# A first transfer of 512 bytes a partition for w_in, and one transfer instead of two for half of wq

## The chip, the cores and the metric

The kernel runs on one core of one Trainium2 chip. The metric is the device time of one execution in microseconds (us); several runs are made, and their median counts.

## What is computed

One decode step of a block that joins sliding-window attention with a gated MLP. Two batch rows of one token, model width 512, 32 query heads over 8 key/value heads of width 128, and a window of the last W = 4096 positions of a cache of 32768. All data are float32.

```python
def reference(A_x, A_k_cache, A_v_cache, A_wq, A_wo, B_x, B_w_in, B_w_sp, B_b_sp, B_w_out):
    x = A_x                                   # 2 x 1 x 512
    xn = _layernorm(x)
    s = _A_ref(xn, A_k_cache, A_v_cache, A_wq, A_wo)
    g = _silu(_B_ref(xn, B_w_in, B_w_sp, B_b_sp, B_w_out))
    return x + s * g

# _A_ref: q = x @ wq (512 x 4096); softmax(q k^T * Dh**-0.5) v over the last W = 4096
#         positions of k_cache, v_cache; then @ wo (4096 x 512)
# _B_ref: z = gelu(x @ w_in) (512 x 1792); z1, z2 = halves; z2 = layernorm(z2);
#         (z1 * (w_sp * z2 + b_sp)) @ w_out (896 x 512)
```

Nearly all of the data are the window of K and V: 2 x 8 x 4096 x 128 values each, 67 MB together. The weights wq and wo have 8.4 MB each, w_in 3.7 MB and w_out 1.8 MB.

## The kernel before

**Loads.** All large loads are issued from SP's queue, in program order. They go through a ring of four tiles of 32 KB a partition (`slot`, line 111) that w_in, the two halves of wq, the K and V units and wo take in turn; a load into a slot waits until the slot's former contents have been used. First come w_in (line 122, 28,672 bytes a partition), w_out (line 124, into a pool of its own, `kts`, which has two buffers), and wq (lines 127 to 131) as two tiles of two rows of wq a partition: the first tile in one transfer of 32 KB a partition, the second in two transfers of 16 KB. Then K and V follow (`load`, line 146) as 8 units of 4 MB each, and six pieces of wo at the end. ScalarE's queue issues the four tiny loads (x twice, w_sp, b_sp).

**The head of the work.** x is normalised and transposed (xn, xnT). PE multiplies it with w_in as soon as that has landed (z, lines 236 to 248), then transposes z back (zT). `queries(k)` (line 263) multiplies xnT with one row tile of wq, 16 matmul instructions each: queries(0) and queries(1) use the first wq tile, queries(2) and queries(3) the second, and k is the accumulation over PSUM, so that the queries are complete after queries(3). Between them stand the small matmuls of the gating branch (mean, variance). After queries(3) PE multiplies with w_out (y), ScalarE copies the queries out (qs), VectorE transposes them (qx) and masks them (xm), PE spreads them (qa), and `place_queries` (the step `q`) lays them out in qb, which every score needs. The buffers of qs and qx are those of `kts`, which afterwards hold the transposed K.

**The units.** The order of everything afterwards is written out by hand in `ORDER` (lines 27 to 52); each word is a step, and each engine runs its steps in that order. For unit u: `K:u` and `V:u` issue the loads; `T:u.0` to `T:u.7` are the 8 transposes of K on VectorE (STREAM_TRANSPOSE, 128x1024); `shares`, `keep` and `scores` are the score matmuls with a copy on ScalarE between them; `rowmax`, `mg`, `shmax` and `bias` give the softmax's maximum; `exp` and `probs_t` the probabilities and their transpose; `pv` multiplies with V (acc); `evac` and `col` gather the heads. Units overlap: while unit u+1 is transposed, unit u's probabilities and `pv` run. `K:0 K:1 V:0` stand first, then `K:2 V:1` with unit 1, and so on; the last loads are those of `wo:0` and `wo:1`.

**The end.** X, Y and U multiply with wo into `part`, Z adds the last rows of wo into `so`, and two VectorE operations multiply with the gate and add x (`res`).

The helper class `InOrder` records every instruction of PE, DVE, ACT and SP, and so nearly all of them show its line (L65) in the profile; they are told apart by their tiles.

Of the kernel before, what the change touches and what calls it, by code (L numbers as in the profile page):

```python
# [70 lines left out]
def kernel(  # L71
# [14 lines left out]
    pe, dve, act, sp = (InOrder(tc, e) for e in (nc.tensor, nc.vector, nc.scalar, nc.sync))  # L86
# [24 lines left out]
    def slot(name, *shape):  # L111
        return ring.tile([P, *shape], F32, tag="slot", name=name)
# [6 lines left out]
    act.dma_start(xs, x[:, 0, :])  # L119
    win_v = w_in.rearrange("(p k) f -> p k f", p=P)  # L120
    win = slot("win", KT, F)
    sp.dma_start(win, win_v)
    wout = kts.tile([P, FT, D], F32, tag="kts", name="wout")
    sp.dma_start(wout, w_out.rearrange("(p j) d -> p j d", p=P))
    wq_v = wq.rearrange("(p k) f -> p k f", p=P)
    wqt = []
    for a in range(0, KT, 2):
        t = slot(f"wq{a}", 2, HQ * DH)
        for k, n in ((0, 2),) if a == 0 else ((0, 1), (1, 1)):
            sp.dma_start(t[:, k : k + n], wq_v[:, a + k : a + k + n, :])  # L130
        wqt += [t[:, 0], t[:, 1]]

    wb1 = cst.tile([1, 2], F32, tag="wb1", name="wb1")
# [92 lines left out]
    for nj in (8, 16):  # L226
        nx = 32 // nj
        to = cst.tile([P, nj * P // 32 // 4, 4, nx], F32, tag=f"perm{nj}", name=f"perm{nj}")
# [374 lines left out]
    for u in range(NU):  # L603
        p = Unit()
        p.u, p.m, p.kt, p.sh, p.ss, p.s, p.p, p.pT = u, None, {}, {}, {}, {}, {}, {}
        units.append(p)
    for line in ORDER.strip().split("\n"):
        for name in line.split():
            name, at = name.split(":")
            u, _, a = at.partition(".")  # L610
# [34 lines left out]
```

## Time and profile before

| | |
|---|---|
| Median of 3 runs | 216.89 us (216.76 to 216.92) |
| Profiled execution: its own time | 217.29 us |
| Profiled execution: span from the first to the last instruction | 215.5 us |
| Mean granted TensorE clock | 0.825 |
| HBM read | 89.40 MB, 415 GB/s over the span |
| Busy: PE, DVE, ACT | 66%, 59%, 24% of the span |

How it is read: all times inside the profile are in us from the start of the span of that one execution, which took 0.4 us longer than the median run. The 16 DMA engines each work through their own share of every load in the order in which SP issued them, 8 of the 128 partitions' rows each; a load is landed when all 16 are done.

### The profile page before, as it was taken

The page shows a single profiled execution, that of the slowest core. Times are in us where ns is not written, and L with a number is a line of the kernel's source. Part 1 is how long each engine was busy: PE and PEld are TensorE (multiplying, and loading weights), DVE is VectorE, ACT ScalarE, POOL GpSimd, SP SyncE. Part 2 cuts the span into 40 slices and gives each one's busy share as a digit, 9 for nine tenths or more (in the row PEclk, how much of TensorE's full clock was granted, in tenths as well). Part 3 has the DMA queues.
Part 4 walks back from the last instruction along what each step waited for, and adds up shares of the span by engine and source line. Part 5 has one row for each costly group of instructions (what it writes and reads, how often), then busy time and mean ns, then how long its engine had stood idle before and what let it go on. Part 6 is the DMA issues. An engine that isn't in the chain of part 4 may idle for free.

```text
span 215.5 us, 2332 instructions
## 1 busy us (share of the span) xinstructions
PE 143.2 (66%) x900; PEld 48.1 (22%) x900; DVE 126.7 (59%) x218; ACT 51.6 (24%) x129; POOL 4.5 (2%) x17
## 2 busy tenths in 40 slices
PE   0179796833854966964991795389259917987793
PEld 0117622111120221222220231123112201232231
DVE  2611213169899799649928972993698099636011
ACT  5011103300116036033330602142051206142201
POOL 8000000000000000000000000000000000000000
PEclk9999569665998896796697599669755997996999
DMA  7999999999999999999999999999999999999990
GB/s 246 432 443 444 398 429 465 414 458 414 456 408 447 420 426 444 426 443 426 450 420 450 408 441 420 426 450 426 447 415 456 401 456 414 447 426 417 420 374 22
DMA packets 3930, 89.54 MB, mean 416 GB/s; under 512 B 446, under 2 KB 462, under 8 KB 848
## 3 DMA queue, kind: packets, MB, share of 16 engines
q1 hardware_dynamic: 3900, 89.40, 96.8%
q8 instruction: 7, 0.11, 0.2%
q14 instruction: 3, 0.02, 0.0%
q10 hardware_dynamic: 20, 0.01, 0.0%
HBM read 89.40 MB, written 0.00 MB: 415 GB/s over the span
## 4 chain that ended last, share of the span: by engine, by line
DMA 63%; PE 23%; DVE 8%; ACT 3%; issue 1%; ACTq 0%
DMA v<-in_A_v_cache_dram 42%; DMA k<-in_A_k_cache_dram 16%; PE acc L65 10%; DMA win<-in_B_w_in_dram 5%; PE sh L65 5%; DVE kts L65 4%; PE part L65 4%; PE s L65 3%; DVE pT L65 1%; ACT p L65 1%; ACT o L65 1%; DVE gate L65 1%; PE mo L65 1%; ACT ss L65 1%; DVE qb L65 1%
## 5 line engine op out<-in xcount | busy, mean ns | idle before, releaser
L65 DVE STREAM_TRANSPOSE kts<-k 128x1024 f32<-128x1024 f32 x64 | 75.6, 1218 | 29.5 <-DMA k<-in_A_k_cache_dram 29.5
L65 PE MATMUL sh<-kts,qb 128*32 128x512 f32 x256 | 41.6, 775 | 13.2 <-DVE kts L65 9.3
L65 PE MATMUL acc<-v,pT 128*32 128x512 f32 x256 | 37.4, 707 | 8.8 <-DVE pT L65 4.4
L65 ACT ACTIVATE p<-s,nb 128x512 f32<-128x512 f32 x32 | 22.5, 733 | 36.2 <-DVE nb L65 36.2
L65 ACT ACTIVATE ss<-sh 128x512 f32<-128x512 f32 x16 | 9.6, 599 | 59.1 <-PE sh L65 59.1
L65 DVE STREAM_TRANSPOSE pT<-p 128x1024 f32<-128x1024 f32 x16 | 19.6, 1225 | 2.3 <-ACT p L65 2.1
L65 PE MATMUL s<-ss,sums 128*128 128x512 f32 x32 | 18.8, 671 | 2.3 <-ACT ss L65 2.3
L65 PE MATMUL mo<-mg,joint 128*128 128x16 f32 x16 | 4.0, 327 | 23.4 <-DVE mg L65 23.4
L65 PEld LDWEIGHTS acc<-v,pT 128*32 128x32 f32 x256 | 10.5, 145 | 35.1 <-issue 27.0
L65 PEld LDWEIGHTS sh<-kts,qb 128*32 128x32 f32 x256 | 8.8, 126 | 34.2 <-issue 28.8
L65 DVE TENSOR_REDUCE m<-s 128x1 f32<-128x512 f32 x16 | 10.7, 671 | 4.2 <-PE s L65 4.2
L65 PE MATMUL q_ps<-wq,xnT 128*32 128x512 f32 x64 | 10.5, 784 | 3.5 <-DMA wq<-in_A_wq_dram 3.5
L65 ACT ACTIVATE o<-acc,wd 128x128 f32<-128x128 f32 x32 | 9.1, 368 | 15.0 <-PE acc L65 15.0
L65 PEld LDWEIGHTS mo<-mg,joint 128*128 128x128 f32 x16 | 3.2, 250 | 27.2 <-DVE mg L65 24.4
L65 PE MATMUL z<-win,xnT 128*32 128x448 f32 x32 | 5.6, 869 | 4.7 <-DMA win<-in_B_w_in_dram 4.7
L65 PE MATMUL part<-wo,oT 128*32 128x512 f32 x56 | 7.7, 596 | 1.4 <-ACT o L65 1.4
L65 PEld LDWEIGHTS s<-ss,sums 128*128 128x128 f32 x32 | 5.0, 197 | 10.3 <-issue 7.7
L65 PE MATMUL zT_ps<-rowm,z 128*128 128x2 f32 x28 | 6.6, 370 | 0.0
L65 PEld LDWEIGHTS zT_ps<-rowm,z 128*128 128x128 f32 x28 | 6.5, 325 | 0.0
L65 ACT ACTIVATION_READ_ACCUMULATOR p<-s,nb 128x1 f32 x32 | 6.5, 203 | 0.0
L65 ACT ACT_TABLE_LOAD x4 | 5.1, 1283 | 2.6 <-POOL hT L164 2.6
L65 DVE COPY z<-z 128x448 f32<-128x448 f32 x2 | 1.3, 626 | 7.5 <-PE z L65 7.5
(111 smaller groups left out, 68.4 us busy)
## 6 DMA issues: line engine op xcount, KB each, us to landing
k<-in_A_k_cache_dram SPq DMA_DIRECT2D x8, 4096.0 KB, 27.4
v<-in_A_v_cache_dram SPq DMA_DIRECT2D x8, 4096.0 KB, 29.8
wq<-in_A_wq_dram SPq DMA_DIRECT2D x1, 4096.0 KB, 24.5
wq<-in_A_wq_dram SPq DMA_DIRECT2D x2, 2048.0 KB
wo<-in_A_wo_dram SPq DMA_DIRECT2D x1, 4096.0 KB, 30.4
win<-in_B_w_in_dram SPq DMA_DIRECT2D x1, 3584.0 KB, 11.5
wo<-in_A_wo_dram SPq DMA_DIRECT2D x1, 2048.0 KB
wout<-in_B_w_out_dram SPq DMA_DIRECT2D x1, 1792.0 KB, 15.3
```

Source lines behind the costliest of these rows:

```text
L65: return self.tc.keep_in_program_order(call(*args, **kwargs))
```

## The change

w_in's load becomes two transfers from the same queue: the first moves the first 128 floats (512 bytes) of every partition's row, the second the other 28,160 bytes. The second tile of wq, which was loaded in two transfers of 16 KB a partition, is loaded in one of 32 KB. The number of transfers stays the same, and so do all other instructions and their order.

```diff
     win_v = w_in.rearrange("(p k) f -> p k f", p=P)
     win = slot("win", KT, F)
-    sp.dma_start(win, win_v)
+    FIRST = 128
+    of, to = win_v.rearrange("p k f -> p (k f)"), win.rearrange("p k f -> p (k f)")
+    sp.dma_start(to[:, :FIRST], of[:, :FIRST])
+    sp.dma_start(to[:, FIRST:], of[:, FIRST:])
     wout = kts.tile([P, FT, D], F32, tag="kts", name="wout")
     sp.dma_start(wout, w_out.rearrange("(p j) d -> p j d", p=P))
     wq_v = wq.rearrange("(p k) f -> p k f", p=P)
     wqt = []
     for a in range(0, KT, 2):
         t = slot(f"wq{a}", 2, HQ * DH)
-        for k, n in ((0, 2),) if a == 0 else ((0, 1), (1, 1)):
-            sp.dma_start(t[:, k : k + n], wq_v[:, a + k : a + k + n, :])
+        sp.dma_start(t, wq_v[:, a : a + 2, :])
         wqt += [t[:, 0], t[:, 1]]
```

## The prediction

> **What bounds the kernel now.** I read the page first, then the chain that ended last, then the DMA's share in short windows at both ends of the span, then the timelines of SP's queue, PE and DVE. The page's slices and its queue list say that this is a kernel of loads.
>
> ```profile
> span 215.5 us, 2332 instructions
> ...
> DMA  7999999999999999999999999999999999999990
> GB/s 246 432 443 444 398 429 465 414 458 414 456 408 447 420 426 444 426 443 426 450 420 450 408 441 420 426 450 426 447 415 456 401 456 414 447 426 417 420 374 22
> ...
> q1 hardware_dynamic: 3900, 89.40, 96.8%
> ```
>
> The 16 DMA engines are busy in every slice but the first and the last, and one queue (SP's) fills 96.8% of them. 89.40 MB at the usual 425 GB/s or so is 210 us of the 215.5. Only the ends are left: slice 0 moved 246 GB/s.
>
> The chain that ended last (start, length, what) shows how the rest hangs on this stream:
>
> ```profile
> 0.73 11.48 DMA win<-in_B_w_in_dram
> ...
> 12.23 33.92 DMA k<-in_A_k_cache_dram
> ...
> 150.21 32.33 DMA v<-in_A_v_cache_dram
> 182.54 0.14 issue
> 182.68 1.95 PE acc L65 x16
> ...
> 206.95 3.64 PE part L65 x28
> ...
> 212.61 0.29 DVE res L65
> ```
>
> A V load that was issued at 150.21 lands at 182.54, although 4 MB need only about 10 us of the stream: it stood 22 us behind other loads. From that landing to 212.9 the chain is compute alone. So the end is the place of that load in the stream plus some 30 us, and a stream that runs d us earlier from its start ends the kernel d earlier. The other end of the stream agrees. In windows (columns: stretch, length, busy time with count of PE, PEld, DVE, ACT, POOL, then clock, DMA share, GB/s):
>
> ```profile
> 0.00:1.60 1.60, 0.00 (x0) 0.00 (x0) 0.00 (x0) 0.00 (x0) 1.05 (x10) 1.00 0.00 0
> 1.60:2.60 1.00, 0.00 (x0) 0.00 (x0) 0.95 (x3) 0.04 (x1) 1.00 (x4) 1.00 1.86 463
> 2.60:3.20 0.60, 0.00 (x0) 0.00 (x0) 0.53 (x3) 0.60 (x1) 0.60 (x1) 1.00 0.00 0
> 3.20:4.20 1.00, 0.00 (x0) 0.00 (x0) 0.01 (x1) 0.97 (x3) 1.00 (x4) 1.00 0.94 401
> 4.20:5.20 1.00, 0.00 (x0) 0.00 (x0) 0.00 (x0) 1.00 (x1) 0.81 (x3) 1.00 1.07 459
> ...
> 207.00:209.00 2.00, 2.00 (x18) 0.71 (x20) 0.00 (x0) 0.00 (x0) 0.00 (x0) 1.00 1.00 407
> ...
> 211.00:211.50 0.50, 0.43 (x19) 0.17 (x12) 0.00 (x0) 0.27 (x1) 0.00 (x0) 1.00 0.09 33
> ...
> 211.57 0.65 PE L65 MATMUL so<-wo,oT 128*32 128x128 f32 x16
> ```
>
> The last pieces of wo are still moving after 211, and the matmuls that need them (the last row, from PE's timeline) are PE's last. Both ends of the work are therefore tied to the stream, not to a free engine.
>
> The same rows hold the term on which this prediction turns. A packet is counted in the window in which it starts. In 1.60:2.60 the rate 463 GB/s over 1 us is 463 KB: 16 rows of w_in of 28,672 bytes, one for each DMA engine, and 4 KB of x. They occupy 1.86 x 16 = 29.8 engine-us, so 1.86 us a row. In 4.20:5.20 again 16 rows start (459 KB) and occupy 1.07 x 16 = 17.1, so 1.07 us a row. Between them, from 2.60 to 3.20, no row starts at all. So **each engine's first row costs 0.79 us more than a later one**, a toll that is paid once, at the head of the stream on which all hangs.
>
> **The change part by part.** The SP queue's timeline, and two of the waits on it:
>
> ```profile
> 0.73 0.39 SPq L65 DMA_DIRECT2D win<-in_B_w_in_dram  x1
> 1.18 0.41 SPq L65 DMA_DIRECT2D wout<-in_B_w_out_dram  x1
> 1.63 1.76 SPq L65 DMA_DIRECT2D wq<-in_A_wq_dram  x3
> 12.23 6.27 SPq L65 DMA_DIRECT2D k<-in_A_k_cache_dram  x2
> ...
> 39.53 0.54 SPq L65 DMA_DIRECT2D k<-in_A_k_cache_dram  x1
> 56.46 0.54 SPq L65 DMA_DIRECT2D v<-in_A_v_cache_dram  x1
> ...
> SPq L65 <- DMA win<-in_B_w_in_dram: 8.8, 1, 8.8
> ```
>
> *The head.* A transfer of 128 rows of 512 bytes (64 KB) goes first, and the remaining 28,160 bytes a row follow one issue later: 1.18 - 0.73 = 0.45 us. Before, the bulk's first rows start at about 1.85 (middle of the starts in 1.60:2.60) and lose 0.79, as if the stream had begun at full speed at 2.64. After, the bulk starts at about 1.85 + 0.45 = 2.30 and has 64 KB less to move, 0.15 us at 425 GB/s. If the small rows take the toll during that issue, the stream stands as if begun at 2.30 - 0.15 = 2.15: **0.49 us gained**. If the toll returns on the bulk, it stands at 2.94: 0.30 lost. No row shows a transfer of small rows on all engines ahead of a large one in an empty queue, so these are the two sides; the worst is that each pays the toll in turn (small rows done at 1.85 + 0.79 + 0.15, then 0.79 again, less the 0.15): 3.43, 0.79 lost. A landing needs all 16 engines, and the second rows start over more than 1 us (14 of the 16, 401 KB, in 3.20:4.20, the others later), so the slowest engine pays about 0.5 more than the mean; if that goes as well, the gain is 1.0. I take -0.6: the mean toll with a little of the spread, since the toll looks tied to the first data, not to the row's length: from the second row on the rate is full at once.
>
> By the Trainium skill, "DMA: Bandwidth & Descriptors", section "Rules for kernel authors", small transfers are to be coalesced, and under 64 KB one pays mostly overhead; its table of measured bandwidth (another issuing path) gives 0.95 us for 64 KB. By that, as an estimate, the 64 KB would cost 0.80 over their 0.15, and the sum would be 217.7 rather than 216.3. No run here shows such a transfer yet.
>
> *The number of rows.* w_in adds 128 rows, the merged wq takes 128 away; five transfers stand ahead of the first K before and after. What a row or a completion costs beside its bytes cancels.
>
> *K:0's issue.* SP waits 8.8 us for w_in's landing before it issues K:0, into a slot that nobody held: of the DMAs in program order (x, w_in, w_out, three of wq, two scalars, x4, K:0) the tenth seems to wait for the second. The count is the same after, so K:0 would wait for the small piece and go out at about 3.5 instead of 12.23. Worth nothing: K:0 lands at 46.15, so its 10 us of data begin near 36. K:1 behind it takes w_in's slot and waits for z's matmuls, as before.
>
> *The queries.* PE and DVE around them, with the total of DVE's waits for K (us, times, longest) as the last row:
>
> ```profile
> 12.35 5.56 PE L65 MATMUL z<-win,xnT 128*32 128x448 f32 x32 [4.73 <-DMA win<-in_B_w_in_dram]
> ...
> 26.18 3.64 PE L65 MATMUL q_ps<-wq,xnT 128*32 128x512 f32 x16 [1.43 <-DMA wq<-in_A_wq_dram]
> ...
> 32.68 1.92 PE L65 MATMUL q_ps<-wq,xnT 128*32 128x512 f32 x16
> ...
> 36.69 2.79 PE L65 MATMUL q_ps<-wq,xnT 128*32 128x512 f32 x16 [2.09 <-DMA wq<-in_A_wq_dram]
> 39.24 2.79 PE L65 MATMUL y<-wout,hT 128*32 128x512 f32 x14
> 44.27 1.12 PE L65 MATMUL qa<-xm,same 128*128 128x256 f32 x2 [2.25 <-DVE xm L65]
> ...
> 46.17 1.25 DVE L65 STREAM_TRANSPOSE kts<-k 128x1024 f32<-128x1024 f32 x1 [2.05 <-DMA k<-in_A_k_cache_dram]
> 47.34 1.19 DVE L65 TENSOR_TENSOR qb<-qa,grpm 128x1024 f32<-128x1024 f32 x1
> ...
> 75.42 3.50 DVE L65 STREAM_TRANSPOSE kts<-k 128x1024 f32<-128x1024 f32 x3 [1.41 <-DMA k<-in_A_k_cache_dram]
> ...
> 94.75 3.50 DVE L65 STREAM_TRANSPOSE kts<-k 128x1024 f32<-128x1024 f32 x3 [3.89 <-DMA k<-in_A_k_cache_dram]
> ...
> DVE kts L65 <- DMA k<-in_A_k_cache_dram: 29.5, 7, 6.7
> ```
>
> queries(2) runs at 32.68 on the first half of the second wq tile; queries(3) waits for the other half until 36.69. Merged, both wait until about 36.7. PE then has 16 matmuls more to do behind the landing: 1.92 us at the pace of 32.68, 3.64 at that of 26.18. Queued behind them on PE are y and qa; SP's K:2 at 39.53 waits for the last one too. qa ends at 45.39, and would end at 47.3 to 49.0; qb starts at 47.34 because DVE is busy with the first transpose of K:0. So qb slips by 0 to 1.7 us and the transposes behind it with it. That slip dies at DVE's next waits for K: 1.41 us at 75.42, 3.89 at 94.75. The loads issued late are covered as well: K:2 (39.53 plus up to 3.6) lands at 75.4 and its data start 10 us before; V:1 (56.46 plus up to 1.7) comes behind K:2 in the stream. Price nil. Without that cover the whole 1.7 would reach the end.
>
> *Sum.* The profiled execution took 217.29 us, its span 215.5 and 1.8 around it; the median of the runs is 216.89, 0.4 lower. 217.29 - 0.6 = 216.7 for a profiled execution, **216.3 for the median**.
>
> **The rivals.** *The toll returns (slower).* The small transfer is through before the bulk's rows are there, the engines start from an empty queue a second time, and the bulk is one issue late: +0.30 to +0.79, 217.2 to 217.7, middle 217.4. For it: in an empty queue every engine paid, all 16 alike, and 64 KB are 0.15 us of work against an issue slot of 0.45, so the queue does run dry if the small rows go at full speed. Against it: then the small rows paid nothing, and a queue that was in use 0.2 us before isn't a cold one. It decides from the point where the bulk loses over 0.49 us on its first rows. The rule named above speaks for this side.
>
> *Nothing moves.* The slow stretch up to about 3 us is fixed in time, whatever is in the queue (no row starts from 2.60 to 3.20); the small piece and the later issue both lie inside it: 216.9, 0.15 either way. The landings then keep their places.
>
> *The queries' slip isn't absorbed.* If PE runs both queries and y at its slow pace and DVE's waits for K vanish, up to 1.7 us reach the end: 218.6. Against it stand DVE's seven waits for K, 29.5 us in all, the longest 6.7: the slip would have to outlast each of them.
>
> **How the numbers follow.** The three runs before lie within 0.07%; 0.2%, 0.43 us, is about what a measurement can tell. Toll absorbed 0.44 (all of it faster by over 0.2%). Toll returns 0.38: about a third of it, 0.12, below +0.43, so 0.26 slower. Nothing moves 0.14. Slip not absorbed 0.04. Hence faster 0.44, same 0.26, slower 0.30. The forecast's own range is 215.8 to 216.45 (-1.1 to -0.43); with the other cases on both sides holding over half the chance, the range goes to 217.6, which leaves out the dearest end of the returning toll and the slip.
>
> **What would show it.** Right: in windows at the head, 64 KB of small rows near 1.6 to 1.9, then rows of 28,160 bytes at 1.05 us each from about 2.3, and no empty stretch like 2.60:3.20; z's matmuls start some 0.5 us before 12.35; the DVE waits for K at 75.42 and 94.75 end 0.5 earlier, and the V landing that was at 182.54 also. K:0's issue stands near 3.5, queries(2) and (3) run back to back from about 36, and that leaves no mark after 95. Wrong: the bulk's first rows again at 1.8 us (the toll returned), z later than 12.35; or landings that moved while the end did not, which would mean that the last 30 us aren't tied to the stream.

## The result, and the profile after

| | Median | Range | Runs |
|---|---|---|---|
| Before | 216.85 us | 216.60 to 216.98 | 13 |
| After | 217.21 us | 216.97 to 217.84 | 13 |

The changed kernel is slower by 0.36 us, by the medians; the ratio of the runs is 1.0021 (+0.46 us) with a 95% interval of 1.0012 to 1.0029, which is +0.26 to +0.63 us. That is inside the stated range and on the other side of the forecast of -0.6: the rival "the toll returns" is what happened, at the low end of its price.

The profiled execution of the changed kernel took 217.06 us with a span of 215.3; that of before took 217.29 with 215.5. Taken alone, these two would say "faster". But before's profiled execution was slower than the slowest of its 13 runs, and one profiled execution against another can't show 0.2%. The sign comes from the medians, and the profiles serve for the places.

SP's queue and PE after the change:

```profile
0.73 0.86 SPq L65 DMA_DIRECT2D win<-in_B_w_in_dram  x2
1.63 0.50 SPq L65 DMA_DIRECT2D wout<-in_B_w_out_dram  x1
2.18 1.28 SPq L65 DMA_DIRECT2D wq<-in_A_wq_dram  x2
3.51 14.39 SPq L65 DMA_DIRECT2D k<-in_A_k_cache_dram  x2
...
12.51 4.78 PE L65 MATMUL z<-win,xnT 128*32 128x448 f32 x32 [4.88 <-DMA win<-in_B_w_in_dram]
```

w_out is issued at 1.63 instead of 1.18, one slot of 0.45 us later, so w_in's bulk went out near 1.18. K:0 is out at 3.51 instead of 12.23. z starts at 12.51 instead of 12.35. The head in windows (stretch, length, PE, PEld, DVE, ACT, POOL, clock, DMA share, GB/s):

```profile
1.60:2.20 0.60, 0.00 (x0) 0.00 (x0) 0.55 (x3) 0.00 (x0) 0.60 (x4) 1.00 0.40 116
2.20:3.20 1.00, 0.00 (x0) 0.00 (x0) 0.93 (x4) 0.61 (x1) 1.00 (x1) 1.00 1.70 451
3.20:4.40 1.20, 0.00 (x0) 0.00 (x0) 0.03 (x1) 1.17 (x3) 1.20 (x4) 1.00 0.61 258
```

The first row holds the small piece: 116 GB/s over 0.6 us is 70 KB (64 KB of w_in and x), in 0.40 x 0.6 x 16 = 3.8 engine-us (us summed over the 16 engines), about 30 ns for each of the 130 rows. At the full rate worked out below they would take 2.6, so they paid 0.08 us an engine: hardly any toll. In the second row the 16 first rows of the bulk start (451 KB), and they occupy 1.70 x 16 engine-us, 1.70 us each, where at full rate (459 KB in 17.1 engine-us before, 26.8 KB per us and engine) they would take 1.05. The toll is back on them, 0.65 us, and they start some 0.5 us later than before: none starts before 2.20, where 14 of the 16 had started by then (676 GB/s in the same 0.6 us from 1.60, 406 KB). Two signs that the prediction had named for being wrong are there: the bulk's first rows again near 1.8 us (1.70), and z later than 12.35 (12.51; by itself this proves little, since with the merge of wq alone, below, z starts at 12.01). The small piece bought next to nothing.

VectorE's waits for K after the change, against 75.42, 94.75, 114.06 and 133.43 of before where such a wait is shown:

```profile
75.83 3.50 DVE L65 STREAM_TRANSPOSE kts<-k 128x1024 f32<-128x1024 f32 x3 [0.29 <-DMA k<-in_A_k_cache_dram]
95.19 3.50 DVE L65 STREAM_TRANSPOSE kts<-k 128x1024 f32<-128x1024 f32 x3 [4.91 <-DMA k<-in_A_k_cache_dram]
...
172.76 1.25 DVE L65 STREAM_TRANSPOSE kts<-k 128x1024 f32<-128x1024 f32 x1 [6.09 <-DMA k<-in_A_k_cache_dram]
```

K lands 0.41 and 0.44 later. In this pair of executions the last one, at 172.76, is earlier than before's:

```profile
152.73 1.25 DVE L65 STREAM_TRANSPOSE kts<-k 128x1024 f32<-128x1024 f32 x1 [5.24 <-DMA k<-in_A_k_cache_dram]
172.91 1.25 DVE L65 STREAM_TRANSPOSE kts<-k 128x1024 f32<-128x1024 f32 x1 [6.66 <-DMA k<-in_A_k_cache_dram]
```

Between these two waits of before lie 20.2 us, where the other steps from K to K are 19.3 to 19.4 (75.42, 94.75). Before's profiled execution lost some 0.8 us there. What did it isn't shown; it would account for the two spans standing the wrong way round.

The queries after the change, and qb behind them:

```profile
37.10 6.37 PE L65 MATMUL q_ps<-wq,xnT 128*32 128x512 f32 x32 [3.43 <-DMA wq<-in_A_wq_dram]
43.29 1.89 PE L65 MATMUL y<-wout,hT 128*32 128x512 f32 x14
...
48.59 1.23 DVE L65 TENSOR_TENSOR qb<-qa,grpm 128x1024 f32<-128x1024 f32 x1 [0.15 <-PE qa L65]
```

queries(2) and (3) run back to back from 37.10, qb is 1.25 us late (48.59 against 47.34), and 0.29 of VectorE's 1.41 us wait at the third K is left; at the next K it waits 4.91 us.

### The profile page after: what moved, and what is told of

It reads as the page before. It is cut to its first block, busy times and chain, and to the rows that moved or that the text cites. A ratio compares the mean times of both kernels' runs of the same rounds, so it can differ in the third digit from the quotient of the medians.

```text
span 215.3 us, 2332 instructions
## 1 busy us (share of the span) xinstructions
PE 140.4 (65%) x900; PEld 48.0 (22%) x900; DVE 126.7 (59%) x218; ACT 51.6 (24%) x129; POOL 4.5 (2%) x17
## 4 chain that ended last, share of the span: by engine, by line
DMA 55%; PE 20%; DVE 18%; ACT 3%; issue 2%; SPq 1%; DVEq 0%; ACTq 0%
DMA k<-in_A_k_cache_dram 25%; DMA wq<-in_A_wq_dram 16%; DMA wo<-in_A_wo_dram 15%; DVE kts L65 12%; PE sh L65 5%; PE acc L65 4%; PE part L65 4%; PE q_ps L65 3%; PE s L65 2%; ACT p L65 2%; DVE pT L65 2%; DVE m L65 1%; PE y L65 1%; SPq L65 1%; DVE gate L65 1%
## 5 line engine op out<-in xcount | busy, mean ns | idle before, releaser
L65 PE MATMUL acc<-v,pT 128*32 128x512 f32 x256 | 34.9, 663 | 8.6 <-DVE pT L65 4.4
L65 PE MATMUL s<-ss,sums 128*128 128x512 f32 x32 | 17.9, 640 | 2.5 <-ACT ss L65 2.5
L65 PE MATMUL q_ps<-wq,xnT 128*32 128x512 f32 x64 | 12.8, 963 | 5.7 <-DMA wq<-in_A_wq_dram 5.7
L65 PEld LDWEIGHTS mo<-mg,joint 128*128 128x128 f32 x16 | 3.4, 263 | 29.6 <-DVE mg L65 26.8
L65 PE MATMUL z<-win,xnT 128*32 128x448 f32 x32 | 4.8, 733 | 4.9 <-DMA win<-in_B_w_in_dram 4.9
L65 DVE STREAM_TRANSPOSE qx<-qs 128x512 f32<-128x512 f32 x2 | 1.3, 690 | 7.9 <-PE y L65 7.9
```

Source lines behind the costliest of these rows:

```text
L65: return self.tc.keep_in_program_order(call(*args, **kwargs))
```

## The experiments

The differences in us are of the medians, against the runs of the kernel before on the same chip; the interval is that of the ratio, times 216.9. Each version has 5 to 12 runs, the kernel before 15 to 29 beside them. Theory A is the returning toll with the later issue, theory B the merged wq, theory C both in part.

**w_in split, wq as before.** One transfer more than before.

```diff
-        sp.dma_start(t, wq_v[:, a : a + 2, :])
+        for k, n in ((0, 2),) if a == 0 else ((0, 1), (1, 1)):
+            sp.dma_start(t[:, k : k + n], wq_v[:, a + k : a + k + n, :])
```

(against the changed kernel)

> w_in begins with the 512-byte transfer, wq stays in its two 16 KB pieces (one transfer more than before). Theory A (the bulk of w_in is issued one slot of 0.45 us late, 0.15 us of it is used, its first rows pay the toll again): the whole loss is here, +0.3 to +0.4 us against the kernel before, the waits for K end 0.4 later, queries(2) runs at about 33 as before. Theory B (the merged wq is the cause, through queries and qb 1.2 us late): within 0.1 us of the kernel before. Theory C (both in part): about +0.2.

Measured 217.40 against 216.87: +0.53, interval +0.43 to +0.91. The whole loss is in the split of w_in; it is somewhat larger than the 0.3 to 0.4 that theory A gave.

**wq merged, w_in as before.**

```diff
-        for k, n in ((0, 2),) if a == 0 else ((0, 1), (1, 1)):
-            sp.dma_start(t[:, k : k + n], wq_v[:, a + k : a + k + n, :])
+        sp.dma_start(t, wq_v[:, a : a + 2, :])
```

(against the kernel before)

> w_in in one transfer as before, the second wq tile in one transfer. Theory A: 0 against the kernel before (within 0.1 us): qb is late by 1 to 2 us, and the waits for K stand at 75.4 and 94.8 as before. Theory B: +0.3 to +0.4 us. Theory C: about +0.2.

Measured 216.94 against 216.87: +0.07, interval -0.13 to +0.26. Theory B falls. Its profile shows the slip and where it ends: qb starts at 47.91, and VectorE waits for K again at 95.05.

```profile
47.91 1.19 DVE L65 TENSOR_TENSOR qb<-qa,grpm 128x1024 f32<-128x1024 f32 x1
...
95.05 3.50 DVE L65 STREAM_TRANSPOSE kts<-k 128x1024 f32<-128x1024 f32 x3 [3.35 <-DMA k<-in_A_k_cache_dram]
```

That wait ends 0.30 later than before's 94.75 although the kernel is no slower, so a single landing of K carries 0.3 us of scatter from one execution to another. The landings above support the medians; alone they would prove little.

**A first piece of 4096 bytes a partition.** `FIRST = 1024` instead of 128 in the changed kernel.

> As the change, with a first piece of 4096 bytes a partition instead of 512 (512 KB, 1.2 us of the stream, more than the issue slot of 0.45 us). Theory A: the bulk's rows are queued before the engines run out of the first piece, so the later issue costs nothing and the toll is paid once: 0 against the kernel before (within 0.1 us), first K wait back at about 75.4. Theory B: +0.3 to +0.4 as the change. If every separate first transfer costs a fixed sum, whatever its size: +0.3 to +0.4 too, but with the waits for K late.

Measured 216.65 against 216.87: -0.22, interval -0.39 to 0.00. The loss is gone, though the bulk is issued as late as in the change. Whether 0.2 us were gained beyond that is the question of the last experiment. The head in windows:

```profile
1.60:3.35 1.75, 0.00 (x0) 0.00 (x0) 1.40 (x4) 0.78 (x1) 1.75 (x4) 1.00 0.86 241
3.35:4.40 1.05, 0.00 (x0) 0.00 (x0) 0.17 (x2) 1.02 (x3) 1.05 (x4) 1.00 1.16 476
```

The first stretch moves 422 KB (the first piece, mostly) in 24.1 engine-us, 15.7 of which are the bytes at full rate: 8.4, or 0.52 us an engine, is the toll. In the second stretch, where the bulk's first rows start, 500 KB take 19.5 engine-us, 25.6 KB per us and engine: within 5% of full rate. With 4 KB rows the first piece pays the toll, and the bulk doesn't pay again.

**Two pieces of 512 bytes ahead of the bulk.**

```diff
     sp.dma_start(to[:, :FIRST], of[:, :FIRST])
-    sp.dma_start(to[:, FIRST:], of[:, FIRST:])
+    sp.dma_start(to[:, FIRST : 2 * FIRST], of[:, FIRST : 2 * FIRST])
+    sp.dma_start(to[:, 2 * FIRST :], of[:, 2 * FIRST :])
```

(against the changed kernel)

> As the change, with two transfers of 512 bytes a partition one after the other ahead of the bulk. Theory A: the bulk is issued one slot later again, 0.4 to 0.45 us less 0.15 us of bytes: +0.6 to +0.8 us against the kernel before, waits for K at 76.1 or so. Theory B: +0.3 to +0.4 as the change.

Measured 217.78 against 216.87: +0.91, interval +0.59 to +1.13. Each short transfer ahead of the bulk costs about one issue slot of 0.45 (w_out, behind the bulk, is issued at 2.17 instead of 1.18).

**First pieces of 1024, 2048 and 7168 bytes a partition**, `FIRST` = 256, 512 and 1792 in the changed kernel.

> As the change, with a first piece of 1024 bytes a partition (128 KB, 0.31 us of the stream at 425 GB/s). Theory A (loss = issue slot of 0.45 us less what the first piece moves in it): 0.45 - 0.31, about +0.15 us against the kernel before, half of the loss with 512 bytes. If any separate small piece costs a fixed sum: +0.36 as with 512 bytes.

Measured 217.33 against 216.84: +0.49, interval +0.26 to +0.72. A miss for theory A as it was written: bytes moved in the slot should have halved the loss, and the +0.15 lies outside the interval.

> As the change, with a first piece of 2048 bytes a partition (256 KB, 0.62 us, more than the slot). Theory A: 0 against the kernel before, within 0.1 us. If the piece must be far longer than the slot because the toll holds up the first piece's rows too: between 0 and -0.2 like the 4096-byte piece. Fixed sum: +0.36.

Measured 216.82 against 216.84: -0.02, interval -0.26 to +0.13.

> As the change, with a first piece of 7168 bytes a partition (all that the first of the four accumulated rows of w_in needs; 0.9 MB, 2.2 us). Theory A: 0 against the kernel before, within 0.1 us, and the same as the 4096-byte piece within 0.15. If the 4096-byte piece's 0.2 us are a real gain (an earlier first matmul of z, or a smaller toll), this one has it too: -0.2. The first of z's matmuls start near 8 us, before the bulk lands.

Measured 216.67 against 216.84: -0.17, interval -0.33 to +0.07. The loss is a step, not a slope: all of it up to 1 KB a partition (0.31 us of the stream, less than the slot), none from 2 KB (0.62 us, more than the slot). That fits the reading that the engines must not run out of rows before the bulk's rows arrive. It is argued, not shown: the rows themselves get longer with the piece, no version sends a long piece of short rows, and no view here shows a single engine's queue. In the windows of the 1 KB and then the 7 KB kernel:

```profile
2.20:3.20 1.00, 0.00 (x0) 0.00 (x0) 0.93 (x4) 0.65 (x1) 1.00 (x1) 1.00 1.85 470
...
4.40:5.10 0.70, 0.00 (x0) 0.00 (x0) 0.00 (x0) 0.70 (x1) 0.62 (x3) 1.00 1.38 584
```

With 1 KB the stretch in which the bulk starts moves 470 KB in 29.6 engine-us, 15.9 KB per us and engine; with 7 KB it is 409 KB in 15.5, 26.4, full rate. With 2 KB the toll is divided: the 156 KB that start from 1.60 to 2.60 occupy 10.9 engine-us, where full rate is 5.8, and the 537 KB from 2.60 to 3.40, the bulk's first rows among them, 23.8, where it is 20.0. That is 0.32 and 0.24 us an engine.

**The 512-byte piece from ScalarE's queue**, ahead of x; w_in's bulk keeps SP's first issue.

```diff
+    act.dma_start(to[:, :FIRST], of[:, :FIRST])
     act.dma_start(xs, x[:, 0, :])
...
-    sp.dma_start(to[:, :FIRST], of[:, :FIRST])
     sp.dma_start(to[:, FIRST:], of[:, FIRST:])
```

(against the changed kernel; wq stays merged)

> The 512-byte piece is issued from ScalarE's queue ahead of x, so that w_in's bulk keeps SP's first issue at 0.73 us. Theory A: nothing stands ahead of the bulk, no slot is lost: 0 against the kernel before, within 0.1 us, waits for K at 75.4; x lands some 0.4 us later, hidden behind w_in. If a piece of 512-byte rows itself costs (its rows, its completion, a second first row): +0.3 to +0.4 as the change.

Measured 216.81 against 216.84: -0.03, interval -0.24 to +0.13. The 128 small rows and the split itself cost nothing that can be measured. The expectation on x missed by far: x was there at 12.9, not 0.4 us late, and z started at 18.0, as the start of VectorE's first work on x, of z, and of qb show:

```profile
12.90 0.68 DVE L65 BATCH_NORM_STATS2 st<-xs 2x6 f32<-2x512 f32 x1 [10.68 <-DMA xs<-in_A_x_dram]
...
18.01 5.80 PE L65 MATMUL z<-win,xnT 128*32 128x448 f32 x32 [0.26 <-DVE xnT L65]
...
47.82 1.19 DVE L65 TENSOR_TENSOR qb<-qa,grpm 128x1024 f32<-128x1024 f32 x1
```

z 5.7 us later than before left no mark on the time. That is the strongest evidence that the head's compute is covered by the stream.

**x's transfer from SP's queue, ahead of w_in**, which stays in one transfer, in the kernel before.

```diff
-    act.dma_start(xs, x[:, 0, :])
+    sp.dma_start(xs, x[:, 0, :])
```

(against the kernel before)

> The kernel before, with x's small transfer (2 rows of 2 KB) issued from SP's queue ahead of w_in instead of from ScalarE's. w_in stays in one transfer; only its issue comes one slot later, and nothing else of w_in is changed. Theory A (the issue slot ahead of the bulk is what costs, not the 512-byte rows): +0.3 to +0.5 us against the kernel before, since nothing of w_in moves in the slot. If the cost lies in the 128 small rows or in the split of w_in: 0.

Measured 217.40 against 216.91: +0.49, interval +0.22 to +0.65. Two rows of 2 KB ahead of w_in cost as much as 128 rows of 512 bytes: it is the slot. SP's queue and the window of w_in's first rows:

```profile
0.73 0.36 SPq L65 DMA_DIRECT2D xs<-in_A_x_dram  x1
1.16 0.36 SPq L65 DMA_DIRECT2D win<-in_B_w_in_dram  x1
...
2.10:3.10 1.00, 0.00 (x0) 0.00 (x0) 0.84 (x3) 0.88 (x1) 1.00 (x1) 1.00 1.91 459
```

w_in is issued at 1.16, and its 16 first rows take 1.91 us each: the full toll, 0.43 us later.

**The control: x from SP's queue behind w_in.**

```diff
-    act.dma_start(xs, x[:, 0, :])
...
     sp.dma_start(win, win_v)
+    sp.dma_start(xs, x[:, 0, :])
```

(against the kernel before)

> Control for the run with x ahead of w_in: x's transfer is issued from SP's queue too, but behind w_in, so that w_in keeps the first issue slot. Theory A (what stands ahead of the bulk costs): 0 against the kernel before, within 0.1 us; x lands behind w_in's first rows, z starts later, hidden as with the piece from ScalarE's queue. If moving x to SP's queue costs by itself: +0.4 to +0.5 as with x ahead.

Measured 217.00 against 216.93: +0.07, ratio 1.0000, interval -0.20 to +0.20. The queue isn't the cause, the place is.

**A first piece of 4096 bytes, wq in its two pieces**, in the kernel before: the candidate for a kernel faster than both.

> The kernel before with a first piece of 4096 bytes a partition and wq in its two 16 KB pieces: the candidate for a kernel faster than both. If the 4096-byte piece's -0.2 us are real (the stream stood 0.1 to 0.2 us earlier in the trace): -0.15 to -0.25 against the kernel before. If they are noise of about 0.1%: within 0.1 us.

Measured 216.94 against 216.91: +0.03, interval -0.26 to +0.11. The 0.2 us of the 4 KB piece did not come back. No version here is shown to be faster than the kernel before.

**The landings of all traces, one execution of each.** The start of queries(0) on PE shows when the first wq tile has landed. It stands at 26.40 (the change), 26.45 (w_in split alone), 26.51 (1 KB), 26.50 (x ahead of w_in) and 26.80 (two small pieces), the five versions that lose time, and at 26.18 (before), 25.86 (wq merged alone), 25.96, 26.02 and 25.70 (2, 4 and 7 KB) and 25.72 (4 KB with wq in two pieces), which don't; with x late (x behind w_in, or behind the small piece) PE isn't ready in time to show it. So the early stream is sorted as the medians are. The later landings of K are not: with 2 KB VectorE's waits end at 75.85 and 95.19, as late as in the change (75.83 and 95.19), though no time is lost. What held that execution's K up isn't shown.

## Why the prediction was wrong, point by point

**What bounds the kernel: right.** The time follows the stream's start. Compute at the head moved by up to 5.7 us without effect, one issue slot ahead of the bulk cost 0.49, two cost 0.91.

**The step that failed** is in the part on the head: "since the toll looks tied to the first data, not to the row's length: from the second row on the rate is full at once". That sentence chose the mean of -0.49 and a little more over the +0.30 that stood beside it. The small rows took 30 ns each and almost no toll (0.08 us an engine), and left it to the bulk, 0.65 us of it, which came one issue slot of 0.45 us later besides: a measured loss of 0.36 instead of the gain of 0.6. The full rate from the second row on showed only that an engine with rows queued pays nothing more; it said nothing on an engine that has only short rows, or that runs out of them and starts anew. The row that decided stood in the text and was used for the rival alone: 64 KB are 0.15 us of work against a slot of 0.45. With 4 KB a partition the first piece does take the toll (0.52 us an engine), with 2 KB a good half of it, and even there the time only equals that of before: the slot spent on issuing the bulk was not lost, and no gain is shown.

**The rival's sum.** 0.45 - 0.15 = +0.30 was stated; +0.36 was measured, +0.53 with wq left alone. The credit of 0.15 for the 64 KB isn't borne out, though the change's own interval would allow it: with 1 KB a partition the same sum gives +0.14 and +0.49 was measured, and a slot in which nothing of w_in moves costs +0.49 too. The measured losses with 0, 64 and 128 KB ahead agree within their intervals with the bare slot, 0.45.

**The rival "nothing moves": not borne out.** The slow stretch isn't fixed in time. With x ahead of w_in the first rows of w_in start from 2.10 on and still take 1.91 us each, and the time goes up with them, by 0.49; with two small pieces it goes up by 0.91.

**The Trainium skill's rule.** The Trainium skill, "DMA: Bandwidth & Descriptors", section "Rules for kernel authors", says that small transfers should be coalesced and pay mostly overhead under 64 KB. It pointed to the right side. The 0.95 us for 64 KB in the table of the same page of the Trainium skill (section "Bandwidth", another issuing path) does not fit here: the small rows occupied 3.8 engine-us, 0.24 us an engine, and where they came from another queue they cost nothing (-0.03). By the measurement the price is that of the place ahead of the bulk.

**The queries: right.** The slip was put at 0 to 1.7 us for qb and nil for the end; it was 1.25, and the merge alone cost +0.07 (-0.13 to +0.26).

**K:0's issue: right, and worth nothing.** It stands at 3.51 against "about 3.5". In the kernel with w_in split and wq as before, which has one transfer more, K:0 is the eleventh DMA, and SP waited 8.5 us for w_in's bulk, the third, again:

```profile
SPq L65 <- DMA win<-in_B_w_in_dram: 8.5, 1, 8.5
```

That kernel lost 0.53 with K:0 at 12.44, and the merge alone lost nothing with K:0 at 2.70, so the early K:0 isn't the cause of the loss. The counting itself doesn't hold everywhere: with x on SP's queue ahead of w_in, K:0 is the tenth and w_in the second as before, and K:0 went out at 3.68, when w_in hadn't landed (z starts at 12.61). What the wait goes by stays open.

**Rows and completions: right.** The count that cancels was no part of the loss: the kernel with a 4 KB piece and wq in two pieces has 128 rows and one transfer more than before, and costs +0.03 (-0.26 to +0.11).

## What to carry to other kernels

In a kernel bound by one stream of loads, what is issued ahead of the first large load counts by its issue slot (here 0.45 us), not by its bytes: put the large load first, and small ones behind it or on another queue, as long as no one waits for them. If the first load must be split, make the first piece longer in the stream than the next issue takes (here from 2 KB a partition on, against 1 KB); that an engine's empty queue, and not its short rows, makes the difference is the likely reason and wasn't tested apart. And a start-up toll that a profile shows is gained back only if something can run under it; find what, with its size, before pricing its removal.

## What the runs showed of the hardware

The first long rows into an empty queue, or behind short rows, cost 0.65 to 0.84 us more than later ones: 1.70 us against 1.05 in the change, 1.91 behind x and 1.86 before against 1.07. Rows of 512 bytes showed hardly any such toll (0.08 us an engine), rows of 4 KB 0.52.

A tiny transfer that stands behind rows of a full stream can be very late. x, two rows of 2 KB, was used from 2.15 us on before; behind the small piece on ScalarE's queue it came at 12.90, and behind w_in on SP's queue VectorE waited for it until 11.81:

```profile
2.15 0.68 DVE L65 BATCH_NORM_STATS2 st<-xs 2x6 f32<-2x512 f32 x1
...
11.81 0.68 DVE L65 BATCH_NORM_STATS2 st<-xs 2x6 f32<-2x512 f32 x1 [9.59 <-DMA xs<-in_A_x_dram]
```

On SP's queue that is the order of issue. On ScalarE's, 8 rows of the small piece an engine stood ahead of x, and the windows of that kernel show how they went:

```profile
3.20:4.20 1.00, 0.00 (x0) 0.00 (x0) 0.00 (x0) 1.00 (x1) 1.00 (x4) 1.00 1.07 459
```

In this microsecond 459 KB start, and the same in each of the next two: 16 rows of 28,160 bytes are 451, and 16 rows of 512 are the other 8. The engines took one row from each queue in turn. 8 such pairs at 1.07 us are 8.6 us, an estimate that covers most of the 10.68 us that VectorE waited for x.
